# Attention scores leave PSUM through the VectorE instruction that finds their extreme, and the exponential runs in SBUF

## The chip, the cores and the metric

The kernel runs on one NeuronCore of a Trainium2 chip. The metric is the device time of one execution in microseconds (us), as the median of three runs. A core has a matrix engine (TensorE, PE in the profile; its weight loads are PEld), a vector engine (VectorE, DVE), an activation engine (ScalarE, ACT), a general engine (GpSimd, POOL) and a queue engine that issues transfers (SyncE, SP). Each engine works through its own instructions in order; they wait for each other by semaphores. PE writes its results to PSUM, from where DVE and ACT take them; SBUF is the working memory.

## The reference, cut to what matters

```python
# q, k, v: (4, 8, 1152, 64); x is (4, 576, 512)
q_pool = q.reshape(B, H, S // 2, 2, D).mean(axis=3)
scores = (1 / np.sqrt(D)) * np.matmul(q_pool, k.transpose(0, 1, 3, 2))
scores = scores - np.max(scores, axis=-1, keepdims=True)
attn = np.exp(scores)
attn = attn / (np.sum(attn, axis=-1, keepdims=True) + 1e-09)
x = np.matmul(attn, v)            # heads side by side: (4, 576, 512)
xn = (x - mean(x)) / sqrt(var(x) + 1e-06) * g_ln
out = x + np.maximum(xn @ w_ch1, 0.0) @ w_ch2   # 512 -> 2048 -> 512
```

## The kernel before, in words

Heads are handled in 16 pairs. A pair has nine steps (`C = 9`), so there are 144 steps, numbered `i`; a step is one block of 128 pooled queries against all 1152 keys. The operands are split into a high and a low fp16 part, so that three fp16 products stand for one exact one.

Two slots of three PSUM banks hold the scores of two successive steps (`slot(i)`, by `i % 2`). `step(i)` writes out the order of the work by hand, the same for all engines:

- `emit_max(i)`: DVE reduces the 1152 scores of each of the 128 rows to their maximum, `mx` (line 390). From step 36 on DVE also makes `nb`, minus the maximum times the scale (line 395).
- `emit_exp(i)`: ACT takes the scores out of PSUM, scales them by `sc` and adds `nb` as the bias, and writes the exponentials, `pe`, to SBUF in fp32 (line 404). In the first 36 steps (`on_pe`) ACT makes `nb` itself just before (line 401).
- `emit_s(i + 1)`: PE computes the scores of the next step into the other slot (lines 371 and 379).
- In the first 36 steps PE transposes `pe` (`emit_t`, line 437) back into the slot that the scores of the step had, ACT copies the result out in the next step (line 443), and PE multiplies it with the values (`emit_pv`, line 461).
- From step 36 on ACT makes the high part of `pe` (`emit_hi`, line 418) and DVE the low part one step later (`emit_lo`, line 427); in three of nine steps POOL makes the low part instead (lines 240 and 425). A DMA transposes both, and PE multiplies them with the values some steps later (line 470). `pe` has two buffers in turn.

Between these lie the preparation of the next pair (PE transposes of k and q, ACT makes the high part, line 275, DVE the low part, line 272), the conversion of the weights (in the first steps on ACT and DVE, then splits on POOL, lines 240 and 794), and, as soon as rows of x are complete, the units of the dense layers (PE lines 621 and 653, with ACT line 634 and DVE line 635 behind the first). After step 143 only dense layers are left.

`scales(p, ...)` computes the powers of two for a pair; `sc[:, 0:1]` is the factor of the exponential and `sc[:, 1:2]`, for the first four pairs, its negative. `qt` holds the two fp16 parts of the transposed queries.

Of the kernel before, what the change touches and what calls it, by code (L numbers as in the profile page):

```python
# [9 lines left out]
FP32 = mybir.dt.float32  # L10
FP16 = mybir.dt.float16
BF16 = mybir.dt.bfloat16
I32 = mybir.dt.int32
ACTF = mybir.ActivationFunctionType
ALU = mybir.AluOpType
AX = mybir.AxisListType
# [8 lines left out]
def tile_pooled_attention_moe(  # L25
# [18 lines left out]
    nc = tc.nc  # L44
    B, H, S, D = q.shape
# [3 lines left out]
    C = S // 128  # L49
# [13 lines left out]
    const = ctx.enter_context(tc.tile_pool(name="const", bufs=1))  # L63
    raw_p = ctx.enter_context(tc.tile_pool(name="raw", bufs=1))
    tr_p = ctx.enter_context(tc.tile_pool(name="tr", bufs=2))
    p_p = ctx.enter_context(tc.tile_pool(name="pp", bufs=2))
    pt_p = ctx.enter_context(tc.tile_pool(name="pt", bufs=5))
    x_p = ctx.enter_context(tc.tile_pool(name="x", bufs=2))
    sm_p = ctx.enter_context(tc.tile_pool(name="sm", bufs=2))
# [17 lines left out]
    wexp = const.tile([128, 4], FP32, name="wexp")  # L87
    wscl = const.tile([128, 4], FP32, name="wscl")
    inv12 = const.tile([128, 2], FP32, name="inv12")
    both = const.tile([128, 2], FP32, name="nhalf")  # L90
    nhalf, eps = both[:, 0:1], both[0:65, 1:2]

# [30 lines left out]
    def load_q(p, engs):  # L123

        b, hp = divmod(p, HP)
        r = raws[p, "q"] = raw_p.tile([128, C, 2, D], FP32, tag="qr", name="qr", bufs=3)
        for h in range(2):
            engs[h % len(engs)].dma_start(
                out=r[64 * h:64 * h + 64],
                in_=q[b, 2 * hp + h].rearrange("(p c r) d -> p c r d", c=C, r=2),  # L130
            )

    pair = {}

    def state(p):
        if p not in pair:
            pair[p] = {
                x: sm_p.tile([128, 3], FP32, tag=x, name=x, bufs=3)
                for x in ("acc", "e", "s", "sc")
            }  # L140
        return pair[p]
# [9 lines left out]
    def qt_of(p):  # L151
        st = state(p)
        if "qt" not in st:
            st["qt"] = tr_p.tile([128, 2, 1280], FP16, tag="qt", name="qt")
        return st["qt"]

    def pool_q(p, eng):
# [3 lines left out]
    def dup_q(p, eng):  # L161
        x = raws[p, "q"]
        eng.tensor_copy(x[:, :, 1], x[:, :, 0])
# [57 lines left out]
    def scales(p, top, a=0, b=3):  # L221

        st = pair[p]
        e, s, sc = (st[x] for x in ("e", "s", "sc"))
        v = nc.vector
        ei, si = (x.bitcast(I32)[:, a:b] for x in (e, s))
        ti = top.bitcast(I32)
        v.tensor_scalar(ei, ti, EXPO, None, op0=ALU.bitwise_and)
        v.tensor_scalar(si, ti, EXPO, EXPO, op0=ALU.bitwise_and, op1=ALU.bitwise_xor)
        if a == 0:  # L230
            v.scalar_tensor_tensor(
                sc[:, 0:1], e[:, 0:1], 2.0 ** -6, e[:, 1:2], op0=ALU.mult, op1=ALU.mult
            )
            if on_pe(p * C):
                v.scalar_tensor_tensor(
                    sc[:, 1:2], e[:, 0:1], -(2.0 ** -6), e[:, 1:2], op0=ALU.mult, op1=ALU.mult
                )

    def scaled(dst, src, s=1.0):
        nc.gpsimd.tensor_scalar(dst, src, s, 1.0, op0=ALU.mult, op1=ALU.mult)  # L240
# [28 lines left out]
    def split_from(what, ps, s, hi, lo):  # L269

        def low():
            nc.vector.scalar_tensor_tensor(lo, ps, s, hi, op0=ALU.mult, op1=ALU.subtract)  # L272
            have.add(what)

        return (lambda: nc.scalar.activation(out=hi, in_=ps, func=ACTF.Copy, scale=s), low)  # L275
# [31 lines left out]
    def prep_q(p, u):  # L307

        qr, qt, s = raws[p, "q"], qt_of(p), pair[p]["s"]
        ps = bank()  # L310
        z = p % HP // 2
        if u == 2:
            nc.tensor.transpose(ps[:, 0:128], qr[:, C - 1].rearrange("p r d -> p (r d)"), ident)
            o, n = 512, 128
            hi, lo = (qt[:, a, o:o + n] for a in range(2))
            return split_from((p, "q", u), ps[:, 0:n], s[:, 1:2], hi, lo)

        d = (256, 128)[z]
        rows = ps.rearrange("p (a h n) -> p a h n", h=2, n=d)
        for c in range(4):  # L320
            a, n = (0, 64 * c) if z == 0 else (c // 2, 64 * (c % 2))
            nc.tensor.matmul(
                out=rows[:, a, :, n:n + 64], lhsT=qr[:, 4 * u + c].rearrange("p r d -> p (r d)"),
                rhs=ident.rearrange("p (h n) -> p h n", h=2), is_transpose=True, start=True, stop=True,
            )
        if z == 0:

            ps = ps.rearrange("p (h n) -> p h n", h=2)
            hi, lo = (
                qt[:, a, 0:1280].rearrange("p (h n) -> p h n", h=2)[:, :, 256 * u:256 * u + 256]  # L330
                for a in range(2)
            )
        else:
            hi, lo = (qt[:, a, 640 * u:640 * u + 512] for a in range(2))
        return split_from((p, "q", u), ps, s[:, 1:2], hi, lo)
# [9 lines left out]
    def on_pe(i):  # L345

        return 0 <= i < HP * C
# [36 lines left out]
        steps[i] = {"s": sp[:, 0:S]}  # L384

    def emit_max(i):
        st = steps[i]
        mx = sm_p.tile([128, 1], FP32, tag="mx", name="mx")
        nb = st["nb"] = sm_p.tile([128, 1], FP32, tag="nb", name="nb")
        nc.vector.tensor_reduce(mx, st["s"], axis=AX.X, op=ALU.max)  # L390
        sc = pair[i // C]["sc"]
        if on_pe(i):
            st["mx"] = mx
        else:
            nc.vector.tensor_scalar(nb, mx, sc[:, 0:1], -1.0, op0=ALU.mult, op1=ALU.mult)

    def emit_exp(i):
        st = steps[i]
        st["pe"] = p_p.tile([128, S], FP32, tag="pe", name="pe")
        if on_pe(i):  # L400
            nc.scalar.activation(
                out=st["nb"], in_=st["mx"], func=ACTF.Copy, scale=pair[i // C]["sc"][:, 1:2]
            )
        nc.scalar.activation(  # L404
            out=st["pe"], in_=st["s"], func=ACTF.Exp,
            scale=pair[i // C]["sc"][:, 0:1], bias=st["nb"],
        )

    pts = {}

# [131 lines left out]
    def bank():  # L542
        for _ in range(2):
            for _ in free_banks:
                nbank[0] += 1
                n = nbank[1] = free_banks[nbank[0] % len(free_banks)]
                if n not in held and n not in waiting:
                    waiting.add(n)
                    return psum[:, n]
            n = nbank[0] + 1  # L550
            while free_banks[n % len(free_banks)] in held:
                n += 1
            release(free_banks[n % len(free_banks)])
# [504 lines left out]
    with tc.manual_schedule():  # L1058
        def now(fn, *a, **k):
            fn(*a, **k)  # L1060

        load_q(0, (nc.sync, nc.scalar))
        load(0, "k", nc.sync)
        load_q(1, (nc.sync,))
        load(0, "v", nc.sync)
        nc.sync.dma_start(out=gsb, in_=g_ln.rearrange("(k p) -> p k", p=128))
        nc.vector.memset(nhalf, -0.5)
        nc.vector.memset(both[:, 1:2], 0.0)
        nc.vector.memset(both[64:65, 1:2], 1e-9)
        for n in (2, 5):  # L1070
            nc.vector.memset(psum[:, n, 386:387], TINY)
        nc.vector.memset(diag, 0.0)
        nc.vector.memset(ones, 2.0 ** -13)
        nc.scalar.activation(out=wexp[:, 0:1], in_=nhalf, func=ACTF.Exp)
        make_identity(nc, ident)

        warm(110)
        st = state(0)
        nc.vector.memset(st["acc"], 0.0)
        pool_q(0, nc.vector)  # L1080
        dup_q(0, nc.gpsimd)
        bound(0, "q")

        nc.scalar.activation(
            out=kt_of(0).rearrange("p a h n -> p (a h n)")[:, 0:C * D],
            in_=raws[0, "k"][:, 0, 0:C].rearrange("p c d -> p (c d)"), func=ACTF.Abs,
            accum_out=st["acc"][:, 0:1],
        )
        nc.vector.tensor_reduce(
            st["acc"][:, 2:3], raws[0, "k"][:, 1, 0:C], axis=AX.XY, op=ALU.max,  # L1090
            apply_absolute_value=True,
        )
        nc.vector.tensor_tensor(st["acc"][:, 0:1], st["acc"][:, 0:1], st["acc"][:, 2:3], op=ALU.max)
        one, two = all_max(st["acc"][:, 0:2], 2, lambda ps: scales(0, ps, 0, 2))
        one()()
        two()()
        free_banks[:] = [6, 7, 3, 4]
        parts = [fn(0, u) for fn, u in PREPS[0][:3]]
        for hi, lo in parts:
            hi()  # L1100
            lo()
        warm(16)
        emit_s(0)
        preps.extend((fn, 0, u) for fn, u in PREPS[0][3:])
        free_banks[:] = [6, 7]
        for h in range(2):
            take_v(0, h)
        i = 0
        while i < NSTEP + 20 or units or evacs or norms:
            step(i)  # L1110
            i += 1
# [29 lines left out]
```

## Time and profile before

| | |
|---|---|
| median of 3 runs (lowest to highest) | 820.64 us (819.19 to 821.6) |
| the profiled execution, its own time | 819.03 us |
| its span on the core | 816.9 us |
| busy: PE, PEld | 783.9 us (96%), 553.2 us (68%) |
| busy: DVE, ACT, POOL | 611.1 us (75%), 559.9 us (69%), 341.3 us (42%) |

The span runs from the first to the last instruction of the core; 2.1 us of the execution lie outside it. Busy times are unions over an engine's instructions. They are averages over stages that differ: attention steps with PE transposes up to about 175 us, attention steps with DMA transposes and dense units up to about 695 us, dense units alone after that. Ends of matmuls are modelled, so a busy PE isn't a PE at its peak.

### The profile page before, as it was taken

Reading aid. Unit: us, or ns where it says so; the run is one execution under the profiler, and the core shown is the slowest. Engines: PE = TensorE matmul, PEld = TensorE weight load, DVE = VectorE, ACT = ScalarE, POOL = GpSimd, SP = SyncE. Lnnn points to the kernel's source line nnn. Section 1 sums busy time; section 2 is a strip of 40 time slices with the busy share of each in tenths; the row PEclk is TensorE's granted clock in tenths of the full one; section 3 lists DMA queues with packets and bytes.
Section 4 is the critical chain, followed back from the end, with each engine's and each line's share of the span. In section 5 each row is a group of like instructions: output and inputs, shape, how many; then the busy total and the mean of one; then the engine's idle time right before and its main releaser. Section 6 shows DMA issues by size and latency. Waiting matters only on the chain.

```text
span 816.9 us, 21326 instructions
## 1 busy us (share of the span) xinstructions
PE 783.9 (96%) x8978; PEld 553.2 (68%) x8978; DVE 611.1 (75%) x1141; ACT 559.9 (69%) x824; POOL 341.3 (42%) x338
## 2 busy tenths in 40 slices
PE   8899999989989999999999999999999999999997
PEld 7687888767566666657566666666675757766764
DVE  4598999899989887898887888888787877521221
ACT  4899998987786868687868786787778676211010
POOL 2010242389999963475452534527252423200000
PEclk9999999999999999999999999999999999999999
DMA  5837465208699999998998989895979687401001
GB/s 145 246 96 262 155 186 149 72 10 172 114 192 158 183 160 205 171 194 150 204 159 185 172 183 169 166 195 111 227 131 211 127 145 124 79 1 27 14 1 26
DMA packets 276016, 115.94 MB, mean 142 GB/s; under 512 B 259280, under 2 KB 259280, under 8 KB 275920
## 3 DMA queue, kind: packets, MB, share of 16 engines
q1 hardware_dynamic: 275840, 114.29, 68.6%
q8 instruction: 70, 1.15, 0.6%
q10 hardware_dynamic: 80, 0.29, 0.2%
q14 instruction: 26, 0.21, 0.1%
HBM read 46.14 MB, written 4.72 MB: 62 GB/s over the span
## 4 chain that ended last, share of the span: by engine, by line
PE 64%; DVE 16%; ACT 10%; POOL 6%; issue 2%; DMA 2%; SPq 0%; POOLq 0%; ACTq 0%; DVEq 0%
PE psum L653 19%; PE psum L621 18%; PE psum L371 7%; PE psum L470 7%; DVE mx L390 5%; ACT pe L404 4%; DVE hl L427 3%; PE psum L461 3%; PE psum L437 2%; PE psum L379 2%; DVE kt L272 1%; DMA vr<-in_v_dram 1%; ACT pt L443 1%; DVE qr L159 1%; POOL wsl L240 1%
## 5 line engine op out<-in xcount | busy, mean ns | idle before, releaser
L404 ACT ACTIVATE pe<-psum,nb,sc 128x1152 f32<-128x1152 f32 x144 | 188.6, 1309 | 33.6 <-DVE r L518 17.6
L390 DVE TENSOR_REDUCE mx<-psum 128x1 f32<-128x1152 f32 x144 | 194.3, 1349 | 15.5 <-PE psum L470 4.5
L653 PE MATMUL psum<-wsl,ht 128*128 128x512 f16 x864 | 196.6, 379 | 7.0 <-DVE ht L635 4.8
L621 PEld LDWEIGHTS <-wsl 128*128 128x128 f16 x1920 | 169.6, 98 | 19.3 <-issue 1.1
L621 PE MATMUL psum<-xn,wsl 128*128 128x256 f16 x1536 | 176.3, 273 | 0.8 <-DVE ht L635 0.6
L653 PEld LDWEIGHTS <-ht 128*128 128x128 f16 x864 | 81.1, 97 | 95.5 <-issue 7.4
L418 ACT ACTIVATE hl<-pe 128x1152 f16<-128x1152 f32 x108 | 125.6, 1163 | 3.4
L634 ACT ACTIVATE ht<-psum 128x512 f16<-128x512 f32 x72 | 42.8, 595 | 123.4 <-PE psum L621 123.3
L371 PE MATMUL psum<-kt,qt 64*128 64x512 f16 (+1 forms) x960 | 119.9, 381 | 3.9 <-ACT pt L443 1.8
L427 DVE SCALAR_TENSOR_TENSOR hl<-pe,hl 128x1152 f16<-128x1152 f32 x72 | 116.3, 1616 | 0.0
L470 PE MATMUL psum<-vt,pt 128*128 128x65 f16 (+2 forms) x3240 | 106.8, 194 | 0.3 <-DMA pt<-hl 0.2
L470 PEld LDWEIGHTS <-pt 128*128 128x128 f16 (+1 forms) x3240 | 98.3, 100 | 3.2 <-DMA pt<-hl 0.6
L635 DVE SCALAR_TENSOR_TENSOR ht<-psum,ht 128x512 f16<-128x512 f32 x72 | 49.5, 688 | 66.1 <-ACT ht L634 65.7
L240 POOL TENSOR_SCALAR pe<-pe 128x1152 f32<-128x1152 f32 x36 | 43.3, 1204 | 120.1 <-ACT hl L418 120.1
L425 POOL TENSOR_TENSOR hl<-pe,hl 128x1152 f16<-128x1152 f32 x36 | 87.0, 2418 | 3.0
L461 PE MATMUL psum<-pt,vt 128*65 128x128 f32 (+1 forms) x720 | 77.4, 263 | 1.3 <-DVE kt L272 1.3
L461 PEld LDWEIGHTS psum<-pt,vt 128*65 128x65 f32 x720 | 71.4, 138 | 1.6 <-DVE kt L272 1.5
L371 PEld LDWEIGHTS <-qt 64*128 64x128 f16 (+1 forms) x960 | 31.9, 96 | 50.3 <-issue 31.7
L379 PEld LDWEIGHTS <-qt 128*128 128x128 f16 (+1 forms) x320 | 17.5, 99 | 63.0 <-issue 62.8
L246 POOL COPY gate<-gate 128x1 f32<-128x1 f32 x27 | 5.0, 184 | 112.5 <-DVE gate L245 112.5
L272 DVE SCALAR_TENSOR_TENSOR qt<-psum,s,qt 128x512 f16<-128x512 f32 (+1 forms) x48 | 29.5, 614 | 29.6 <-ACT qt L275 28.9
L667 DVE SCALAR_TENSOR_TENSOR xb<-psum,inv,xb 128x512 f32<-128x512 f32 x32 | 23.8, 744 | 35.6 <-PE psum L653 35.5
(115 smaller groups left out, 996.7 us busy)
## 6 DMA issues: line engine op xcount, KB each, us to landing
stage<-in_moe_w_ch_dram SPq DMA_DIRECT2D x32, 512.0 KB, 6.6
kr<-in_k_dram SPq DMA_DIRECT2D x16, 576.0 KB, 4.5
vr<-in_v_dram SPq DMA_DIRECT2D x16, 576.0 KB, 4.9
qr<-in_q_dram SPq DMA_DIRECT2D x31, 288.0 KB, 5.5
out_dram<-xb SPq DMA_DIRECT2D x32, 128.0 KB, 2.4
pt<-hl SPq DMA_TRANSPOSE x108, 5.2
kr<-in_k_dram SPq DMA_DIRECT2D x16, 64.0 KB, 4.2
out_dram<-xh SPq DMA_DIRECT2D x4, 128.0 KB, 2.7
```

The lines of the kernel that those rows point to most:

```text
L240: nc.gpsimd.tensor_scalar(dst, src, s, 1.0, op0=ALU.mult, op1=ALU.mult)
L371: nc.tensor.matmul(out=sp[o:o + w, c0:c0 + 512], lhsT=qt[r:r + 64, qa, q0:q0 + w], rhs=kt[r:r + 64, ka, h], start=(a == 0), stop=(a == 2),)
L390: nc.vector.tensor_reduce(mx, st["s"], axis=AX.X, op=ALU.max)
L404: nc.scalar.activation(out=st["pe"], in_=st["s"], func=ACTF.Exp, scale=pair[i // C]["sc"][:, 0:1], bias=st["nb"],)
L418: nc.scalar.activation(out=hl[:, 0], in_=st["pe"], func=ACTF.Copy, scale=2.0 ** 15)
L425: nc.gpsimd.tensor_tensor(hl[:, 1], st["pe"], hl[:, 0], op=ALU.subtract)
L427: nc.vector.scalar_tensor_tensor(hl[:, 1], st["pe"], 2.0 ** 15, hl[:, 0], op0=ALU.mult, op1=ALU.subtract)
L461: nc.tensor.matmul(out=ps[0:65, q0:q0 + w], lhsT=vt[:, h, c], rhs=pt[:, 128 * u + q0:128 * u + q0 + w], start=(u == 0), stop=(u == C - 1),)
L470: nc.tensor.matmul(out=dst[:, 0:n], lhsT=pt[:, a + u, q0:q0 + w], rhs=vt[:, h, c, x0:x0 + n], start=(u == 0 and a == 0 and n == 65), stop= ...
L621: nc.tensor.matmul(out=ps[:, o:o + n], lhsT=wsl[:, 8 * w + cc, wa, f * 128:f * 128 + 128], rhs=xn[:, xa * KD + cc, 0:n], start=(m == 0), s ...
L635: lambda: nc.vector.scalar_tensor_tensor(lo, pv, 0.0, hi, op0=ALU.max, op1=ALU.subtract),
L653: nc.tensor.matmul(out=ps, lhsT=hv[0][:, ha, f, t * 128:t * 128 + 128], rhs=wsl[:, 8 * w + 4 + f // 2, wa, (f % 2) * DM:(f % 2) * DM + DM] ...
```

## The change

One VectorE instruction (`tensor_tensor_reduce`) reads the scores from PSUM as its first tensor and a zero, repeated along the row, as its second; it adds the two, multiplies by the scale with its sign changed, writes the 1152 results per row to `pe` in SBUF, and writes their minimum to `nb`. It stands where the maximum stood. ACT then computes exp(-1 times `pe` plus `nb`) in SBUF, from `pe` into `pe`. `mx`, the separate computation of `nb` on DVE or ACT, and `sc[:, 1:2]` go. `pe` is now allocated in `emit_max` and has three buffers; the tile for `qt` is shorter by 128 elements a row and its second part is laid out without a gap.

```diff
+    nought = const.tile([128, 1], FP32, name="nought")
...
     def qt_of(p):
         st = state(p)
         if "qt" not in st:
-            st["qt"] = tr_p.tile([128, 2, 1280], FP16, tag="qt", name="qt")
+            x = tr_p.tile([128, 4 * C * 64 + 128], FP16, tag="qt", name="qt")
+            st["qt"] = x[:, 0:4 * C * 64].rearrange("p (a n) -> p a n", a=2)
+            st["qt+"] = x
...
         if a == 0:
             v.scalar_tensor_tensor(
-                sc[:, 0:1], e[:, 0:1], 2.0 ** -6, e[:, 1:2], op0=ALU.mult, op1=ALU.mult
+                sc[:, 0:1], e[:, 0:1], -(2.0 ** -6), e[:, 1:2], op0=ALU.mult, op1=ALU.mult
             )
-            if on_pe(p * C):
-                v.scalar_tensor_tensor(
-                    sc[:, 1:2], e[:, 0:1], -(2.0 ** -6), e[:, 1:2], op0=ALU.mult, op1=ALU.mult
-                )
...
             hi, lo = (
-                qt[:, a, 0:1280].rearrange("p (h n) -> p h n", h=2)[:, :, 256 * u:256 * u + 256]
+                pair[p]["qt+"][:, 1152 * a:1152 * a + 1280].rearrange("p (h n) -> p h n", h=2)[
+                    :, :, 256 * u:256 * u + 256
+                ]
...
     def emit_max(i):
+
         st = steps[i]
-        mx = sm_p.tile([128, 1], FP32, tag="mx", name="mx")
+        st["pe"] = p_p.tile([128, S], FP32, tag="pe", name="pe", bufs=3)
         nb = st["nb"] = sm_p.tile([128, 1], FP32, tag="nb", name="nb")
-        nc.vector.tensor_reduce(mx, st["s"], axis=AX.X, op=ALU.max)
-        sc = pair[i // C]["sc"]
-        if on_pe(i):
-            st["mx"] = mx
-        else:
-            nc.vector.tensor_scalar(nb, mx, sc[:, 0:1], -1.0, op0=ALU.mult, op1=ALU.mult)
+        nc.vector.tensor_tensor_reduce(
+            out=st["pe"], in0=st["s"], in1=nought[:, 0:1].to_broadcast([128, S]),
+            scale=pair[i // C]["sc"][:, 0:1], scalar=3.0e38, op0=ALU.add, op1=ALU.min, accum_out=nb,
+        )
 
     def emit_exp(i):
         st = steps[i]
-        st["pe"] = p_p.tile([128, S], FP32, tag="pe", name="pe")
-        if on_pe(i):
-            nc.scalar.activation(
-                out=st["nb"], in_=st["mx"], func=ACTF.Copy, scale=pair[i // C]["sc"][:, 1:2]
-            )
-        nc.scalar.activation(
-            out=st["pe"], in_=st["s"], func=ACTF.Exp,
-            scale=pair[i // C]["sc"][:, 0:1], bias=st["nb"],
-        )
+        nc.scalar.activation(out=st["pe"], in_=st["pe"], func=ACTF.Exp, scale=-1.0, bias=st["nb"])
...
         nc.vector.memset(nhalf, -0.5)
+        nc.vector.memset(nought, 0.0)
```

## Rows read from the trace of the kernel before

**Rows 1.** Windows: stretch, length, busy us (x instructions) by engine, PEclk, DMA, GB/s

```profile
14.00:170.00 156.00, 149.11 (x1440) 121.83 (x1438) 132.02 (x293) 139.96 (x241) 39.42 (x65) 1.00 0.49 153
170.00:300.00 130.00, 119.80 (x1428) 82.70 (x1425) 118.85 (x198) 99.34 (x137) 120.22 (x90) 1.00 0.81 149
300.00:700.00 400.00, 391.58 (x5069) 261.60 (x5068) 326.21 (x583) 301.30 (x411) 175.50 (x165) 1.00 0.91 169
```

**Rows 2.** The same windows for the maximum alone (line 390, DVE)

```profile
14.00:170.00 156.00, 47.34 (x35) 1.00 0.49 153
170.00:300.00 130.00, 36.34 (x27) 1.00 0.81 149
300.00:700.00 400.00, 110.61 (x82) 1.00 0.91 169
```

**Rows 3.** Timeline of the first stage: start, us, engine, line, [idle before <-releaser]

```profile
89.46 1.35 DVE L390 TENSOR_REDUCE mx<-psum 128x1 f32<-128x1152 f32 x1
...
90.73 0.15 DVE L516 RECIPROCAL r<-psum 64x2 f32<-64x2 f32 x1
90.85 0.29 ACT L401 ACTIVATE nb<-mx,sc 128x1 f32<-128x1 f32 x1 [0.20 <-DVE mx L390]
...
91.18 1.31 ACT L404 ACTIVATE pe<-psum,nb,sc 128x1152 f32<-128x1152 f32 x1
...
93.13 1.15 PE L437 MATMUL psum<-ident,pe 128*128 128x128 f32 x9
...
93.34 0.75 DVE L272 SCALAR_TENSOR_TENSOR kt<-psum,s,kt 128x512 f16<-128x512 f32 x1 [0.31 <-ACT kt L275]
...
94.02 1.35 DVE L390 TENSOR_REDUCE mx<-psum 128x1 f32<-128x1152 f32 x1
```

**Rows 4.** Line 404: first what it waited for, then who waited for it (us, times)

```profile
  POOL hl L425: 7.1, 6
...
  PEld psum L437: 6.1, 9
```

**Rows 5.** Timeline at 228 us, POOL's low part and what follows it

```profile
228.40 2.37 POOL L425 TENSOR_TENSOR hl<-pe,hl 128x1152 f16<-128x1152 f32 x1
...
230.80 1.31 ACT L404 ACTIVATE pe<-psum,nb,sc 128x1152 f32<-128x1152 f32 x1 [1.99 <-POOL hl L425]
...
231.91 1.34 DVE L390 TENSOR_REDUCE mx<-psum 128x1 f32<-128x1152 f32 x1
232.16 0.82 PE L371 MATMUL psum<-kt,qt 64*128 64x512 f16 x6 [0.88 <-ACT pe L404]
```

**Rows 6.** Groups of DVE by form: busy us, mean ns | idle before, releasers

```profile
L635 DVE SCALAR_TENSOR_TENSOR ht<-psum,ht 128x512 f16<-128x512 f32 x72 | 49.5, 688 | 66.1 <-ACT ht L634 65.7
L272 DVE SCALAR_TENSOR_TENSOR qt<-psum,s,qt 128x512 f16<-128x512 f32 x32 | 24.0, 749 | 21.9 <-ACT qt L275 21.6
...
L395 DVE TENSOR_SCALAR nb<-mx,sc 128x1 f32<-128x1 f32 x108 | 23.1, 214 | 3.8
```

**Rows 7.** Line 427: duration in ns, least, median and most

```profile
L427 DVE SCALAR_TENSOR_TENSOR hl<-pe,hl x72: 1347/1350/3133, 184.9 to 691.1; 128x1152 f16<-128x1152 f32 x72
```

**Rows 8.** Timeline at 440 us: DVE's pair, and an ACT instruction with an accumulator

```profile
440.28 1.36 DVE L390 TENSOR_REDUCE mx<-psum 128x1 f32<-128x1152 f32 x1 [1.04 <-PE psum L470]
...
441.80 0.21 DVE L518 TENSOR_SCALAR r<-psum,s 128x1 f32<-128x1 f32 x1
...
446.49 1.15 ACT L179 ACTIVATE kt<-kr 128x1152 f16<-128x1152 f32 x1
...
447.55 0.19 ACT L179 ACTIVATION_READ_ACCUMULATOR kt<-kr 128x1 f32 x1
```

**Rows 9.** Groups of ACT by form: busy us, mean ns | idle before, releasers

```profile
L404 ACT ACTIVATE pe<-psum,nb,sc 128x1152 f32<-128x1152 f32 x144 | 188.6, 1309 | 33.6 <-DVE r L518 17.6 <-POOL hl L425 7.1 <-DVE nb L395 5.6
L418 ACT ACTIVATE hl<-pe 128x1152 f16<-128x1152 f32 x108 | 125.6, 1163 | 3.4
```

**Rows 10.** Windows for line 635 alone (DVE)

```profile
170.00:300.00 130.00, 8.17 (x12) 1.00 0.81 149
```

## The prediction, made before the changed kernel was run

> **What bounds the kernel now.** I read the windows by stage first, because the shares of the whole span mix three kinds of step [rows 1]. From 300 to 700 us PE is busy for 391.6 of 400 us, while DVE has 74 us to spare: whatever the change does to DVE or ACT there can give back at most 8 us and, up to DVE's slack, costs little. After 700 us there are no scores. What can move lies before 300 us. From 14 to 170 us PE is idle for 6.9 of 156 us, and DVE (132) and ACT (140) aren't far behind. From 170 to 300 us PE is idle for 10.2 of 130 us, and DVE (118.9) and POOL (120.2) are the full engines. So the gain of any change to DVE and ACT is bounded by some 17 us of idle PE, and it counts only where a PE wait ends on one of the instructions that it touches.
>
> Next the timeline of one step of the first stage [rows 3]. The reader is to see a loop. DVE finds the maximum at 89.46, ACT makes `nb` and begins the exponential at 91.18, 1.72 us later; ACT then makes the high part of the prepared tile, DVE waits 0.31 us for that and makes the low part at 93.34, and only then, at 94.02, comes the next maximum: a period of 4.56 us, set by neither engine alone. PE, though, transposes at 93.13 without a wait, 0.64 us after the exponential ended at 92.49: here PE is the late one, and a faster loop gives it nothing. The view of line 404's waits says where it would: PE's weight loads waited 6.1 us in 9 places for the exponential before the transposes [rows 4].
>
> Last the waits of the exponential. In six places, 7.1 us, it waited for POOL to give back a buffer of `pe` [rows 4]. One is shown [rows 5]: POOL ends at 230.77, the exponential begins at 230.80, 1.99 us late, and the next scores on PE begin 0.88 us late in their turn, since the exponential still held their PSUM slot.
>
> **The change, part by part.** *The new DVE instruction.* No instruction of this kind is in the trace. Its main part reads 1152 fp32 scores from PSUM and one more input. The reduction takes 47.34/35 = 1.35 us [rows 2]. A three-operand instruction from PSUM with 512 elements takes 0.688 us, the same with a scalar from a tile 0.749 [rows 6], so the scalar costs 0.06; one over 1152 elements takes 1.35 us when nothing stretches it [rows 7]. Main part: 1.35 + 0.06 = 1.41 us. The minimum must then be written out. For that the trace has only ACT's counterpart: 446.49 + 1.15 = 447.64 is the end of the main instruction, 447.55 + 0.19 = 447.74 that of the accumulator's read [rows 8], 0.10 us later. Bounds for the whole: 1.35 us (scalar and read free) and 1.41 + 0.21 = 1.62 us (the read as dear as line 395, with no overlap [rows 6]). I take 1.51, by the ACT read, which is the same act on another engine.
>
> [...]
>
> *What it replaces on DVE.* From step 36 on the pair of maximum and `nb` holds DVE from 440.28 to 441.80, 1.52 us [rows 8]. So DVE is even there: 1.51 for 1.52, within -0.17 and +0.10 a step. In the first 36 steps the next DVE instruction began 1.27 us after the maximum did (89.46 to 90.73 [rows 3]); there DVE pays 0.24 us a step more.
>
> *What it removes on ACT.* In the first 36 steps `nb` goes: from its start to the exponential's is 0.33 us (90.85 to 91.18 [rows 3]). The exponential now reads SBUF with one scalar from a tile. The same length from SBUF without any takes 1.163 us, from PSUM with two 1.309 [rows 9]; these are the bounds, and I take 1.26, nearer the upper, since it keeps its bias: 0.05 us less. ACT is relieved by 0.38 us a step in the first stage and by 0.05 after.
>
> *The loop of the first stage.* Maximum to exponential: 1.72 becomes about 1.51 + 0.06 = 1.57; the exponential gives 0.05 more. The loop goes from 4.56 to 4.36 us. But DVE's own work in that step is 4.56 - 0.31 = 4.25 us, and with 0.24 more it is 4.49. So DVE becomes the limit of such a step, and of the 0.20 only 0.07 is left. Over the stage PE has 149.1/35 = 4.26 us a step and DVE 132.0/35 = 3.77 [rows 1, 2], with the new instruction 4.01: PE stays the fuller engine on average, so DVE's extra work is covered by PE's. If that cover were gone, 35 x 0.24 = 8.4 us would be to pay.
>
> What remains as a gain is where PE waited for the exponential: 9 places, 6.1 us [rows 4]. Each place can give back what the path before it lost: 0.20 by the loop alone, 0.38 where ACT was the full engine. 9 x 0.25 = 2.2 us, with 0.9 and 3.4 as ends; I take off 0.3 for steps in which DVE had no idle time: -1.9 us.
>
> *170 to 300 us.* DVE is even, 27 steps x (-0.17 to +0.10) = -4.6 to +2.7 us, taken as zero. The PSUM slot is now free when DVE is done with it, not after the exponential; the wait of 0.88 us for it goes [rows 5], and the third buffer takes away ACT's waits for POOL, 7.1 us [rows 4], of which little reaches PE, since the exponential's readers have steps to spare. Together -1.0 us, between 0 and -4.
>
> *A wait that is added.* The new instruction must find a free `pe`; behind it on DVE stand the reciprocals for the finished rows and the low parts that PE's dense units read. It needs the buffer of three steps before. In the tight case shown the buffer was given back at 230.77, and the third step's maximum began at 231.91 [rows 5]: 1.14 us to spare, so no price; if POOL's queue were later by more, the 2.37 us of line 425 would be the size of the stall.
>
> *The rest.* One memset, four small DVE instructions less, another layout of `qt` with the same instructions: nothing, hidden in DVE's 24 us of slack in the first stage [rows 1].
>
> *Sum.* -1.9 - 1.0 = -2.9 us against the profiled execution's 819.03: 816.1. The median stands 1.6 us above it, so 820.64 - 2.9 = 817.7 us.
>
> **The rivals.**
>
> *Hidden anyway.* PE has no more than these few waits, and the places that are released early wait next for the dense units' low parts. For it: PE transposes 0.64 us after it could [rows 3]. Against it: nine waits that end on the exponential. Then -0.5 to +1.5 us: 820.9.
>
> *All waits are paid back.* The nine waits (6.1 us) go, and a third of PE's 10.2 idle us from 170 to 300 with them (3.4): -9 us, 811.6. For it: ACT's relief of 0.38 us a step is larger than what most of the waits measure. Against it: DVE takes 0.24 of it back in the same loop.
>
> *Slower: the hand-over of the minimum.* If main part and read together take the upper bound or more, DVE becomes the limit before 300 us. It decides from 1.52 us on in the second stage, where DVE is busy for 91% [rows 1], and from 1.27 + 0.31 = 1.58 on in a regular step of the first. At 1.62: 27 x 0.10 + 26 x 0.04 = 3.7 us (26 are the first stage's 35 less the 9 with a wait), and of the gains about 0.5 left: +3, 823.6. Every further 0.1 us costs some 53 x 0.1 = 5 us. For it: no row of this kind. Against it: the ACT pair overlaps.
>
> *Half rate.* If two inputs, a written result and a running minimum together went at half the elements per unit of time, 1152 x (1.350 - 0.688)/640 = 1.19 us more a step [rows 6, 7]: DVE would be the limit everywhere. 35 x 1.19 + 27 x 1.19 = 74 us before 300 us, less some 25 of DVE's idle 24 + 11 there; after it 82 x 1.19 = 98 less the 74 of slack, of which perhaps half can be used: about +50 + 60, 930 us. Against it: line 427 has two inputs of the same length and is at full rate [rows 7]. [...]
>
> A stretch by POOL, which takes line 427 up to 3.13 us [rows 7], I count with the slower cases at a very small chance: line 635, with one input in PSUM and one in SBUF as the new one has, took 8.17/12 = 0.68 us while POOL was busy for 92% [rows 1, 10], no more than its mean.
>
> **How the numbers follow.** Forecast 0.50, hidden anyway 0.16, all waits paid 0.14, hand-over 0.16, half rate 0.04. The forecast's own range is -0.5 to -5.5 us (the ends of its terms, partly offset): 815.1 to 820.1. A measurement of this kernel tells about 0.3%, 2.5 us, from no change. Three fifths of the forecast lie beyond that, with all of the faster rival: 0.44. Slower: half rate and four fifths of the hand-over: 0.17. Within: 0.39. The range goes from 812, which leaves out half of the faster rival, to 826, which leaves out half rate and the dearer part of the hand-over.
>
> **What the profile after would show.** The new line at about 1.41 us, with a short read right behind it, and 1.5 us from its start to the next DVE instruction; line 404's successor near 1.26 us and no line 401; the exponential 1.57 us after the new instruction's start in the first stage; PE's waits for the exponential down from 6.1 us to about 4; no wait of ACT for POOL's low part, and none of DVE in its place; DVE's busy time from 14 to 170 us up by some 8 us; the stretch from 300 to 700 us unchanged in length. The prediction is wrong if the new instruction with its read takes over 1.6 us, if DVE waits for `pe`, or if PE's idle time before 300 us doesn't fall.

## The result, and the profile after

| | before | after |
|---|---|---|
| median (lowest to highest) | 819.91 us (819.12 to 821.6, 4 runs) | 812.24 us (811.42 to 813.88, 4 runs) |
| the profiled execution, span | 819.03, 816.9 us | 812.92, 811.1 us |

The ratio is 0.9906, with a 95% interval of 0.9881 to 0.9931: the change makes the kernel 7.7 us, or 0.9%, faster. The direction is the one forecast, but the forecast gain was 2.9 us, and 812.24 us lies outside the forecast's own range (815.1 to 820.1). It is inside the stated range, whose fast end is 812, by 0.24 us, and only because half of the faster rival was taken in; that is luck. Runs of one kernel differ by some 1.5 to 2.5 us with their mean granted clock (after, 811.42 us at 1.000, 812.92 at 0.998 and 813.88 at 0.997); at a mean clock of 1.000 the profiled execution before took 819.03 us and two runs after took 811.42 and 811.56 us, which is nearly the same gain.

The windows of the stages after, in the columns of [rows 1]:

```profile
14.00:170.00 156.00, 151.13 (x1456) 123.94 (x1457) 135.28 (x328) 133.40 (x211) 39.87 (x65) 0.99 0.49 153
170.00:300.00 130.00, 119.54 (x1441) 82.23 (x1439) 116.42 (x198) 96.86 (x134) 121.59 (x90) 1.00 0.85 151
300.00:700.00 400.00, 394.72 (x5097) 263.57 (x5094) 316.79 (x590) 295.71 (x412) 175.68 (x169) 1.00 0.92 170
```

Against [rows 1], PE is 2.0 us busier in the first stretch and 3.1 us in the last, and not busier in the middle. The last stretch is the surprise. DVE's busy time rises by 3.3 us in the first stage, where some 8 was expected, and falls by 9.4 us after 300 us.

The new instruction, as a source view of its line (least, median and most ns of one; then the costliest of what it waited for, and who waited for it, in us and times):

```profile
L392 DVE CUSTOM_DVE_ANT_0 pe<-psum,nought,sc x144: 1384/1412/1419, 14.7 to 684.1; 128x1152 f32<-128x1152 f32 x144
L392 DVE DVE_READ_ACCUMULATOR2_ANT nb<- x144: 76/84/89, 16.1 to 685.4; 128x1 f32 x144
...
  PE psum L462: 7.5, 10
...
  ACT pe L399: 31.0, 33
```

Its main part is the 1.41 us of the forecast, with a longest of 1.419: nothing stretches it. It waits mostly for PE's matmuls (the costliest line is that of the matmuls with the values), and nowhere for POOL. The exponential, now line 399, by the same view and with those who waited for it:

```profile
L399 ACT ACTIVATE pe<-pe,nb x144: 1239/1255/1277, 16.2 to 685.6; 128x1152 f32<-128x1152 f32 x144
...
  PEld psum L429: 2.1, 3
```

It takes 1.255 us in the median, where the mean had been 1.309 [rows 9], and PE's weight loads waited 2.1 us in 3 places for it, where it had been 6.1 us in 9 [rows 4]. It waits for DVE alone; POOL's 7.1 us [rows 4] are gone.

One step of the first stage after, on the timeline, to lay beside [rows 3]:

```profile
89.57 1.42 DVE L392 CUSTOM_DVE_ANT_0 pe<-psum,nought,sc 128x1152 f32<-128x1152 f32 x1
90.91 0.09 DVE L392 DVE_READ_ACCUMULATOR2_ANT nb<- 128x1 f32 x1
90.91 0.16 DVE L508 RECIPROCAL r<-psum 64x2 f32<-64x2 f32 x1
91.03 1.26 ACT L399 ACTIVATE pe<-pe,nb 128x1152 f32<-128x1152 f32 x1 [0.17 <-DVE nb L392]
...
93.29 0.75 DVE L271 SCALAR_TENSOR_TENSOR kt<-psum,s,kt 128x512 f16<-128x512 f32 x1
93.97 1.41 DVE L392 CUSTOM_DVE_ANT_0 pe<-psum,nought,sc 128x1152 f32<-128x1152 f32 x1
```

The reader is to see three starts. The read begins at 90.91, before the main part's end at 90.99, and the reciprocal behind it begins at 90.91 too. Before, the reciprocal also began 0.08 us ahead of the end of the maximum (90.73, where 89.46 + 1.35 = 90.81 [rows 3]), so the read takes nothing of its own here. DVE gets on 1.34 us after the new instruction's start, against 1.27 after the old maximum. The exponential begins 1.46 us after that start, against 1.72. And DVE's low part at 93.29 no longer waits for ACT: the period is 4.40 us, against 4.56.

From step 36 on the same hand-over stands against the old pair of 1.52 us [rows 8]:

```profile
442.32 1.41 DVE L392 CUSTOM_DVE_ANT_0 pe<-psum,nought,sc 128x1152 f32<-128x1152 f32 x1
443.66 0.08 DVE L392 DVE_READ_ACCUMULATOR2_ANT nb<- 128x1 f32 x1
443.66 0.22 DVE L510 TENSOR_SCALAR r<-psum,s 128x1 f32<-128x1 f32 x1
```

That is 1.34 us, so DVE gains some 0.18 us in each of 108 steps.

**Where the time went.** Each step starts with line 390 or its successor on DVE. Subtracting those starts on the two timelines gives the gain by stretch (before, steps 5, 36, 63 and 143 start at 36.36, 178.74, 308.29 and 688.72 us; after, at 37.37, 177.06, 306.18 and 684.09). The same subtraction for the experiments below, each against before, in us:

| stretch | after | e3 | e4 | e5 | e6 | e7 | e8 | e9 | e10 | e11 | e12 |
|---|---|---|---|---|---|---|---|---|---|---|---|
| start to step 5 | +1.0 | +2.2 | -0.8 | +1.7 | -0.3 | +0.2 | +0.5 | +1.2 | +1.7 | +1.5 | 0.0 |
| steps 5 to 36 | -2.7 | -2.4 | -2.6 | +0.4 | -2.6 | +0.1 | -2.7 | -2.7 | -2.7 | -2.3 | +0.1 |
| steps 36 to 63 | -0.4 | -0.2 | +0.4 | +0.8 | +0.3 | -0.4 | -4.4 | -4.5 | -2.7 | -0.3 | -1.1 |
| steps 63 to 143 | -2.5 | -2.0 | +0.5 | -2.5 | +0.3 | -2.6 | -2.9 | -4.2 | -2.3 | -2.5 | +0.7 |
| step 143 to the end | -1.2 | -0.1 | -1.1 | -1.1 | +0.1 | -1.2 | -1.1 | -1.1 | -1.2 | -1.1 | +0.3 |

Each column is one profiled execution. Below the first row, stretches that an edit leaves as they were agree with before within some 0.3 us (e6 from step 36 on, e7 up to it), so a difference of that size is not read as an effect.

The first row is mostly the clock. In the profile after, PE's granted clock was 0.57, 0.50, 0.50 and 0.72 in the four microseconds from 26 to 30 us; before, it kept 1.00 there. The window with the fall, after:

```profile
23.90:30.00 6.10, 4.04 (x20) 2.67 (x20) 2.00 (x5) 5.09 (x10) 0.00 (x0) 0.72 0.99 321
```

PE had waited for ACT just ahead of it, for 2.06 us; at the same place before, where the clock held, it had waited for 1.55 us. First after, then before:

```profile
25.74 0.37 PE L372 MATMUL psum<-kt,qt 64*128 64x512 f16 x1 [2.06 <-ACT pt L435]
```

```profile
25.50 0.37 PE L371 MATMUL psum<-kt,qt 64*128 64x512 f16 x1 [1.55 <-ACT pt L443]
```

Why that wait is longer after was not followed up. The profiles of e4 and e6, which have the new instruction in these steps and no such stretch (granted 1.00 in the mean from 14 to 170 us, against 0.99 after), gain 0.3 to 0.8 us in that row. With about -0.5 there, the sum of the column is -7.3 us, near the measured 7.7.

**The last row** has its place on the timeline. Before, the dense unit behind the last exponential waits for it, since it needs a PSUM bank that the exponential still reads:

```profile
690.45 1.31 ACT L404 ACTIVATE pe<-psum,nb,sc 128x1152 f32<-128x1152 f32 x1
...
691.81 2.75 PE L653 MATMUL psum<-wsl,ht 128*128 128x512 f16 x12 [1.07 <-ACT pe L404]
```

After, the same unit begins while the exponential runs:

```profile
685.64 1.25 ACT L399 ACTIVATE pe<-pe,nb 128x1152 f32<-128x1152 f32 x1
...
686.02 2.76 PE L645 MATMUL psum<-wsl,ht 128*128 128x512 f16 x12
```

### The profile page after: what moved, and what is told of

Same layout as the page of the kernel before. It is cut to its first block, busy times and chain, and to the rows that moved or that the text cites. A ratio compares the mean times of both kernels' runs of the same rounds, so it can differ in the third digit from the quotient of the medians.

```text
span 811.1 us, 21365 instructions
## 1 busy us (share of the span) xinstructions
PE 783.1 (97%) x8978; PEld 553.7 (68%) x8978; DVE 599.3 (74%) x1174; ACT 544.4 (67%) x788; POOL 341.3 (42%) x338
## 4 chain that ended last, share of the span: by engine, by line
PE 67%; POOL 13%; DVE 10%; issue 4%; ACT 3%; DMA 2%; SPq 0%; POOLq 0%; ACTq 0%; DVEq 0%
PE psum L645 19%; PE psum L613 18%; PE psum L372 8%; PE psum L462 7%; PE psum L453 5%; POOL wsl L239 4%; PE psum L429 3%; POOL wsl L786 3%; PE psum L380 2%; POOL hl L417 2%; DVE pe L392 2%; DVE hl L419 1%; DMA vr<-in_v_dram 1%; PE psum L321 1%; PE psum L1048 1%
## 5 line engine op out<-in xcount | busy, mean ns | idle before, releaser
L392 DVE CUSTOM_DVE_ANT_0 pe<-psum,nought,sc 128x1152 f32<-128x1152 f32 x144 | 203.1, 1411 | 17.5 <-PE psum L462 7.5
L399 ACT ACTIVATE pe<-pe,nb 128x1152 f32<-128x1152 f32 x144 | 180.4, 1253 | 31.9 <-DVE nb L392 31.0
```

The costliest lines, as they stand in the source:

```text
L392: nc.vector.tensor_tensor_reduce(out=st["pe"], in0=st["s"], in1=nought[:, 0:1].to_broadcast([128, S]), scale=pair[i // C]["sc"][:, 0:1], s ...
L399: nc.scalar.activation(out=st["pe"], in_=st["pe"], func=ACTF.Exp, scale=-1.0, bias=st["nb"])
```

## The experiments

The pieces to tell apart are the third buffer, the place that the exponential reads (and with it the early release of PSUM), DVE's hand-over, and ACT's `nb`. Diffs are against the changed kernel unless another is named. Each time stands against runs of the kernel before on the same chip (820.7, 820.38 or 819.35 us).

### e1: two buffers of `pe`

```diff
-        st["pe"] = p_p.tile([128, S], FP32, tag="pe", name="pe", bufs=3)
+        st["pe"] = p_p.tile([128, S], FP32, tag="pe", name="pe", bufs=2)
```

> The changed kernel with two buffers for pe instead of three; all else stays. If the third buffer is itself a source of the gain (theory B), half of the 7.7 us is lost: about 816 us. My theory is that the buffer is no gain of its own but a condition: the new instruction takes its buffer at the start of a step, where the exponential took it in the middle, so with two it must wait on DVE for POOL's low part of two steps before. By the times of the trace of before POOL ended that part after the maximum of that step had begun in most of the 36 places, by about 1 us and by up to 5; so DVE would wait some 30 us in all, part of it hidden behind PE: 822 to 840 us, slower than before.

833.62 us (832.59 to 834.9), ratio 1.0165 [1.0149, 1.0181]: slower than before by 13 us. DVE's waits, and the second window:

```profile
DVE pe L392 <- POOL hl L417: 35.6, 22, 5.9
```

```profile
170.00:300.00 130.00, 114.97 (x1316) 78.83 (x1316) 99.56 (x185) 89.59 (x125) 107.00 (x83) 0.95 0.76 140
```

With two buffers it is DVE that waits for POOL's low part, 35.6 us in 22 places, where ACT had waited 7.1 us in 6 [rows 4], and from 170 to 300 us DVE gets through 99.6 us of work, against 116.4 in the changed kernel. PE, busy for 115.0 us there against 119.5, was granted 0.95 of its clock in the mean. The third buffer is a condition of the change.

### e2: three buffers alone

Against the kernel before (with the shorter `qt` of the change; `mx` and `nb` share a tile, for room):

```diff
-        st["pe"] = p_p.tile([128, S], FP32, tag="pe", name="pe")
+        st["pe"] = p_p.tile([128, S], FP32, tag="pe", name="pe", bufs=3)
```

> The kernel before with a third buffer for pe (and the shorter qt that makes room for it), the maximum and the exponential as before. Theory B: 3 us or more faster than before. My theory: ACT's waits for POOL (7.1 us, 6 places) go, but little reaches PE: 0 to 1.5 us faster, not to be told from no change.

819.87 us, ratio 0.9997 [0.9988, 1.0005]: nothing. ACT's 7.1 us for POOL were hidden, as the forecast held for most of them, and the profile has none of them left. By the interval at most 0.12%, 1.0 us, could come from here.

### e3: the exponential from PSUM, as before

```diff
-        nc.scalar.activation(out=st["pe"], in_=st["pe"], func=ACTF.Exp, scale=-1.0, bias=st["nb"])
+        nc.scalar.activation(
+            out=st["pe"], in_=st["s"], func=ACTF.Exp,
+            scale=pair[i // C]["sc"][:, 1:2], bias=st["nb"],
+        )
```

(`sc[:, 1:2]` is the scale with a positive sign. DVE's instruction is unchanged, its written scores unused.)

> The changed kernel, but the exponential reads the scores from PSUM with a positive scale, as before, so it holds the PSUM slot until it ends and takes 0.05 us more; the copy that the new instruction writes is overwritten unread. One small DVE instruction more for each pair. Theory R (the slot that is released early, and the shorter exponential, bring the gain): 3 us or more of the 7.7 are lost, 815 or above. Theory D (DVE's time brings it): under 1 us is lost, 812 to 813.

815.77 us (813.69 to 816.11), 0.994 [0.9926, 0.9954]: by the ratios some 2.8 of the 7.7 us are lost (the 3.5 us of the next run's expectation compare times of two chips). The timeline at its last exponential:

```profile
687.83 1.31 ACT L402 ACTIVATE pe<-psum,nb,sc 128x1152 f32<-128x1152 f32 x1
...
689.19 2.75 PE L651 MATMUL psum<-wsl,ht 128*128 128x512 f16 x12 [1.01 <-ACT pe L402]
```

The dense unit's wait at the end is back, 1.01 us for 1.07, and each other run whose late exponentials read PSUM has it as well (e2, e6 and e12, 1.1 us each); it is absent from every profile in which they read SBUF. So this 1.1 us is shown to come from the bank's early release. Another 1.0 us is spread over the steps (the table), in amounts of 0.2 to 0.5 that hardly stand out. That makes 2.1 us for the edit; the rest of this profile's loss is in its first row, where its clock was the lower one (0.99 granted from 14 to 170 us, 0.997 in the mean).

### e11: the exponential in SBUF, but as long as from PSUM

```diff
-        nc.scalar.activation(out=st["pe"], in_=st["pe"], func=ACTF.Exp, scale=-1.0, bias=st["nb"])
+        nc.scalar.activation(out=st["pe"], in_=st["pe"], func=ACTF.Exp, scale=nought[:, 1:2], bias=st["nb"])
```

(`nought[:, 1:2]` holds -1.)

> The changed kernel with the exponential's factor -1 taken from a tile: it still works in SBUF, but should take about as long as out of PSUM (1.31 us) or up to 1.35. The kernel with the exponential out of PSUM lost 3.5 us. If its longer exponential was the cause, this one loses 3 us or more: 815 to 816. If the slot that is held was the cause, under 1 us: 812 to 813.

813.91 us (812.23 to 816.14), 0.9927 [0.9912, 0.9941]. The group of the exponential (busy us, mean ns):

```profile
L399 ACT ACTIVATE pe<-pe,nb,nought 128x1152 f32<-128x1152 f32 x144 | 193.9, 1347 | 31.0 <-DVE nb L392 30.3
```

It is now longer than before's 1309 ns [rows 9], and yet, outside the first row of the table, it loses 0.6 us where e3 loses 2.1 (0.4 of them from step 5 to 36, and 0.1 at most where e3 loses 1.1, at the end). e3's loss is therefore not mainly one of the exponential's duration; the held bank is the larger part. That rests on one profile of each, since the intervals of the two times overlap.

### e4: DVE's time given back from step 36 on

```diff
-            scale=pair[i // C]["sc"][:, 0:1], scalar=3.0e38, op0=ALU.add, op1=ALU.min, accum_out=nb,
+            scale=pair[i // C]["sc"][:, 0:1], scalar=3.0e38, op0=ALU.add, op1=ALU.min, accum_out=nb if on_pe(i) else mn,
         )
+        if not on_pe(i):
+            nc.vector.tensor_scalar(nb, mn, nought, 1.0, op0=ALU.add, op1=ALU.mult)
```

> The changed kernel with a small DVE instruction behind the new one from step 36 on, which takes the minimum to nb: DVE is again as long as with the pair of before (about 0.2 us a step more, 20 us in all). Theory D: 3 us or more of the gain are lost, 815 to 817. Theory R: under 1 us is lost.

816.89 us (814.98 to 817.48), 0.9961 [0.9948, 0.9975]: some 4 us are lost. The group of the added instruction, then the last window:

```profile
L399 DVE TENSOR_SCALAR nb<-nb,nought 128x1 f32<-128x1 f32 x108 | 23.1, 214 | 3.9
```

```profile
300.00:700.00 400.00, 391.81 (x5068) 261.92 (x5067) 332.25 (x669) 295.71 (x411) 175.24 (x166) 1.00 0.92 169
```

PE falls back to before's 391.6 us [rows 1], and in the table the gain of steps 63 to 143 turns from -2.5 into +0.5, while the stages that the edit does not touch keep theirs. So what comes back after 300 us, apart from the end, hangs on these 0.21 us a step on DVE between the scores and the exponential. With them the hand-over from step 36 on is about as long as the forecast had it, and the gain of the whole is 3.8 us, near its 2.9. The edit adds occupancy and delay at once, and this run does not separate them.

### e5: ACT's `nb` given back in the first 36 steps

```diff
+        nb = st["nb"]
+        if on_pe(i):
+            nb = st["nb2"]
+            nc.scalar.activation(out=nb, in_=st["nb"], func=ACTF.Copy, scale=nought[:, 1:2])
-        nc.scalar.activation(out=st["pe"], in_=st["pe"], func=ACTF.Exp, scale=-1.0, bias=st["nb"])
+        nc.scalar.activation(out=st["pe"], in_=st["pe"], func=ACTF.Exp, scale=-1.0, bias=nb)
```

(Here `nought[:, 1:2]` holds 1.)

> The changed kernel with a small ACT instruction before the exponential in the first 36 steps, like the one that made nb there before: ACT is again 0.3 us a step longer in the first stage. If ACT's relief there brought the drop of PE's waits for the exponential (6.1 to 2.1 us), 2 to 4 us of the 7.7 are lost: 814 to 816. If the shorter path over DVE did it, under 1 us.

820.35 us (818.03 to 822.87, 12 runs), 1.0002 [0.9991, 1.0014]: the whole gain is lost, more than either theory had. What the profile shows of it is smaller: steps 5 to 36 lose 3.1 us against the changed kernel, steps 36 to 63 1.2, and PE's weight loads wait again for the exponential:

```profile
PEld psum L435 <- ACT pe L405: 5.4, 8, 1.1
```

That is near before's 6.1 us in 9 places [rows 4], so the removal of ACT's `nb` from the path is what frees the first stage. (The edit makes ACT busier and the path longer at once; which of the two counts is not separated.) The profiled execution, 818.03 us, is this kernel's fastest, with a mean clock of 0.997; most of the others have 0.996, one 0.994, while the kernel before has 0.998 or 1.000. So the time holds both the longer first stage and more of the lower clock. Why this edit brings more of the lower clock was not followed up.

### e6 and e7: the change in the first 36 steps alone, and from step 36 on alone

```diff
+    def fused(i):
+        return on_pe(i)
```

(That is e6; e7 has `not on_pe(i)`. Where `fused` does not hold, the maximum, `nb` and the exponential from PSUM stand as before; three buffers throughout.)

> The new instruction and the exponential in SBUF only in the first 36 steps; from step 36 on the maximum, nb and the exponential out of PSUM as before (three buffers all along). In the profile of after the steps begin 1.7 us earlier than before by step 36, and the span is 5.8 us shorter. If the gain lies by stage as those starts say, this kernel is 1.5 to 3 us faster than before: 818 to 819. If the first stage has most of it, as my sum had it (1.9 of 2.9), 5 us or more: 815 or below.

> The other half of the split: the new instruction and the exponential in SBUF only from step 36 on, the first 36 steps as before. The kernel with the first half alone was 2.6 us faster than before (ratio 0.9968). If the halves add up, this one is 5 us faster: 815 to 816. If they need each other, less than 3.5 us: 817 or above.

e6: 817.34 us (816.39 to 818.37), 0.9968 [0.9956, 0.998]. e7: 816.17 us (814.76 to 819.21, 12 runs), 0.9961 [0.9948, 0.9973]. In the table each keeps its own stretches and has nothing in the other's. The halves add up to 0.32% + 0.39% = 0.71%; the whole has 0.94%, with an interval from 0.69% on. By its time e7's gain of 3.2 us lies on the side of "they need each other" (under 3.5 us); but its runs differ in their mean clock (0.996 to 1.000), and by the profiles the spans of the two halves, 2.2 and 3.9 us shorter, add up to the whole's 5.8.

### e8, e9, e10: POOL's low parts moved to DVE

POOL is busy for 121.59 of 130 us from 170 to 300 us, and after the change it has a larger share of the chain that ended last. Shares by engine, before:

```profile
PE 64%; DVE 16%; ACT 10%; POOL 6%; issue 2%; DMA 2%; SPq 0%; POOLq 0%; ACTq 0%; DVEq 0%
```

After:

```profile
PE 67%; POOL 13%; DVE 10%; issue 4%; ACT 3%; DMA 2%; SPq 0%; POOLq 0%; ACTq 0%; DVEq 0%
```

So the change's freed DVE time was offered to the low parts that POOL makes in three of nine steps: up to step 63 (e8), in all steps (e9), and up to step 63 for one of the three (e10).

```diff
-        return i % C in (2, 5, 8)
+        return i % C in (2, 5, 8) and i >= 63                 # e8
+        return i % C in (2, 5, 8) and i >= 144                # e9
+        return i % C in ((2, 8) if i < 63 else (2, 5, 8))     # e10
```

> The changed kernel with all low parts of steps 36 to 62 on DVE; POOL makes them from step 63 on as before. POOL was busy for 94% from 170 to 300 us and stands in the chain that ended last with 13%; nine of its low parts (3.6 us each) go to DVE (1.35 us each, 12 us in all, where DVE has 13.6 us of 130 idle). If POOL bounds that stage in the changed kernel, 2 to 4 us faster than it: 808 to 810. If DVE does, 3 us or more slower: 815 or above.

> The changed kernel with all 36 low parts of POOL on DVE. From 300 to 700 us DVE had 83 us idle and takes 27 x 1.35 = 36 us more. If DVE's time still counts there, as the kernel with 0.2 us a step given back says (it lost 4 us for 20 us of DVE), this is 3 to 7 us slower than the kernel with the early ones alone (808.4): 811 to 815. If POOL's stretch of DVE's own low parts was the cost, as fast or faster: 806 to 808.

> The changed kernel with one of three of POOL's low parts of steps 36 to 62 on DVE (three in all), the rest as in the changed kernel. If POOL's load in that stage sets the time in proportion, a third of the 3.9 us that all nine gave: about 811. If one place sets it, all or nothing: 808 or 812.

e8: 808.38 us (806.84 to 809.66), 0.9858 [0.9842, 0.9873]. e9: 807.71 us (807.4 to 807.85), 0.9854 [0.9841, 0.9868]. e10: 811.74 us (808.9 to 812.98), 0.99 [0.9883, 0.9917]. By these times e10 has no gain over the changed kernel that can be told, but its profile has one: from step 36 to 63 it stands at -2.7 us where the changed kernel has -0.4 and e8 -4.4, so one of three moved gives more than half of what all three give. Its first row (+1.7 us, in a profile with a mean clock of 0.997) hides part of that; its one run at a mean clock of 1.000 took 808.9 us, against 811.42 and 811.56. The second window of e8, then the last of e9:

```profile
170.00:300.00 130.00, 123.17 (x1474) 83.92 (x1475) 123.34 (x212) 100.09 (x139) 96.43 (x75) 1.00 0.84 156
```

```profile
300.00:700.00 400.00, 396.55 (x5133) 266.57 (x5130) 347.47 (x619) 295.21 (x412) 80.71 (x112) 1.00 0.90 169
```

In e8 POOL loses 25 us of work there and DVE takes only 7 more, and PE gains 3.6 us: the stretch that the change itself hardly moved moves by 4.4 us against before. In e9 DVE has 31 us more after 300 us than in the changed kernel and PE is busier all the same. That is the side of e9's second theory, and DVE's own low parts are indeed shorter there (1.62 us in the mean in the changed kernel, 1.47 in e9, 1.35 in the median of both); whether that or POOL's lighter load brings the gain is not separated. Both beat both kernels; e9 is the fastest version of this study, 1.5% under the kernel before.

### e12: the same move without the change

Against the kernel before:

```diff
-        return i % C in (2, 5, 8)
+        return i % C in (2, 5, 8) and i >= 63
```

> The kernel before with all low parts of steps 36 to 62 on DVE, nothing else changed. If the freed DVE time of the new instruction is what makes room for them, this gains under 1.5 us or loses: 819 or above. If POOL was the bound in both kernels, it gains about as much as in the changed one, 3 to 4 us: 816 to 817.

818.86 us (817.72 to 821.19, 12 runs), 0.9989 [0.9978, 1.0001]. Its second window:

```profile
170.00:300.00 130.00, 121.83 (x1438) 83.94 (x1434) 122.57 (x204) 100.02 (x138) 94.63 (x75) 0.99 0.79 149
```

By its time the same edit is worth nothing that can be told in the kernel before (0.22% at most), and 3.9 us in the changed one. DVE is as full as in e8 (122.6 and 123.3 us), but in e8 that holds more of the work: 27 steps at 0.18 us less are 4.9 us. The profile shows what became of the move here: it gains 1.1 us from step 36 to 63 and gives 1.0 back after it, and within the gain lies a loss. One of DVE's low parts, beside POOL's work on the weights, lasts 3.32 us; PE waits 1.79 us for the DVE instruction behind it, and the granted clock is 0.66 and 0.50 in the two windows that follow:

```profile
210.77 3.32 DVE L427 SCALAR_TENSOR_TENSOR hl<-pe,hl 128x1152 f16<-128x1152 f32 x1
...
215.33 0.63 PE L576 MATMUL psum<-ident,xs 128*128 128x128 f32 x4 [1.79 <-DVE qt L272]
```

```profile
216.00:218.00 2.00, 2.00 (x30) 1.46 (x27) 1.97 (x4) 1.85 (x2) 1.92 (x3) 0.66 1.16 213
218.00:220.00 2.00, 2.00 (x14) 0.91 (x12) 1.97 (x4) 1.97 (x5) 2.00 (x1) 0.50 0.14 30
```

PE is busy throughout these two windows, so the lower clock costs some 1.7 us (an estimate from these two rows, which takes PE's work to go with the granted clock: 2 x 0.34 + 2 x 0.50). Eleven of e12's twelve runs have a mean clock of 0.994 to 0.998, where 14 of the 23 runs before have 0.999 or 1.000. So in this stretch part of the difference between the profiles of e8 and e12 is the clock, and not room on DVE alone; e8's runs have 0.996 to 0.999, so how much of the difference in time is the clock's stays open. The third buffer and the early release differ as well between the two, so which of these makes the room is not shown.

## Why the prediction came out as it did

The direction, the place of the first gain and most single prices held; the sum was too small by 4.8 us, and that the time is still within the stated range is luck, by 0.24 us.

- *The new instruction's main part*: 1.41 us forecast, 1.412 measured. Neither half rate nor a stretch by POOL appears in 144 instances (1384 to 1419 ns).
- *Its hand-over*: 1.51 us forecast, 1.34 measured, under the lower bound of 1.35. This is the term that was mis-sized. The forecast laid the accumulator's read behind the main part, by ACT's pair [rows 8]. On DVE the read takes 0.08 us, starts 0.06 to 0.09 us before the main part has ended, and the next instruction starts with it. The 0.10 us that the sum had for a read on DVE no run shows; the trace after has the read, in all 144 steps, as a second instruction that keeps DVE no longer (1.34 us to the next instruction, with a main part of 1.41). So DVE pays 0.07 us a step in the first stage and not 0.24, and gains 0.18 a step later where the forecast had it even (its lower bound was -0.17).
- *The first stage*: -1.9 us forecast; -2.7 us measured from step 5 on, and some -0.5 before it. PE's waits for the exponential fell to 2.1 us, not to 4. The forecast's own argument gave it too little, because with 1.51 us DVE would have become the limit of a step (4.49 us); with 1.34 the step shown is 4.40. e5 shows that taking ACT's `nb` out of the path is the part that matters there. The lower end of this term, 0.9 us, follows from neither of its own figures (9 x 0.20 = 1.8, 9 x 0.07 = 0.6).
- *170 to 300 us*: -1.0 us forecast, -0.4 measured. ACT's waits for POOL were indeed hidden (e2), and DVE's gain of 4.9 us did not reach PE. In e8, with POOL's low parts moved, that stretch gains 4.4 us; how much of it is DVE's freed time stays open (e12).
- *After 300 us*: nothing forecast, -2.5 us in the steps and -1.2 at the end measured. The bound "at most 8 us" held; the step that failed is the choice of zero under it, since a DVE step taken as even left nothing to come back. PE's idle 8.4 us were treated as out of reach, but most of them end on DVE: before, of 8.3 us of listed waits from 300 to 700 us, 5.4 are for DVE and 2.5 for ACT. The first three lines (us, times, longest) are

```profile
PE psum L653 <- DVE ht L635: 2.2, 2, 1.3
PE psum L653 <- DVE xb L667: 1.1, 1, 1.1
PE psum L653 <- ACT pe L404: 1.1, 1, 1.1
```

and after, the first two have become (the third is gone)

```profile
PE psum L645 <- DVE ht L627: 1.6, 2, 1.0
...
PE psum L645 <- DVE xb L659: 0.8, 1, 0.8
```

  All listed waits sum to 8.3 us before and 5.1 after; those for DVE fell from 5.4 to 3.6. e4 shows that the 2.5 us hang on the shorter DVE step, and e3 that the third wait, 1.1 us at the end of attention, was one for PSUM. The forecast had seen that release, and had priced it at one place only [rows 5].
- *The third buffer*: no price and no gain of its own, as forecast (e2); that it must be there is e1.
- *The exponential*: 1.26 us forecast, 1.255 measured; 1.57 us after the new instruction's start forecast, 1.46 measured, again by the read. No line 401, no wait of ACT for POOL, and none of DVE in its place, as listed.

Of the rivals, "all waits are paid back" has nearly the size (811.6 us), but not the mechanism: half of the gain lies after 300 us, where it had nothing, and PE's idle time from 170 to 300 us did not fall.

Of the theories weighed in the runs, that of DVE's time and that of the earlier release of PSUM both hold in part: e4 shows the first (2.5 us after step 63), e3 against e11 the second (1.1 us at the end; the 1.0 us at most in the steps is near what two profiles differ by). Neither covers the first stage, which hangs on ACT's `nb` (e5).

What stays open: whether e4 loses by DVE's occupancy or by the later exponential (e9 adds 31 us to DVE after 300 us without a loss, which speaks for the delay, but takes POOL's low parts out as well); which of the changes lets e8 gain what e12 does not, and how much of that is the clock; and why e5 brings more of the lower clock.

## What to carry to other kernels

For an instruction that joins several, work out when the next instruction on its engine and the first consumer can start, not only how long it lasts: here that difference (1.34 against 1.51 us) was most of the forecast's error, as e4 shows, which puts it back from step 36 on and gains 3.8 us. A few us of idle time on the bounding engine are worth listing by what ends them, even in a stage where it is 98% busy: most of those waits ended on the engines that the change relieved. And when an edit frees time on one engine, offer it work from a neighbour that now stands on the chain: the same move was worth 3.9 us with the change, and without it nothing that can be told, where an instruction stretched to 3.32 us and a granted clock of 0.66 and 0.50 over 4 us took back part of it.

## What the runs showed of the hardware that was not expected

- The read of DVE's accumulator took 76 to 89 ns and began 1.34 us after the start of a main part of 1.41 us (medians of 144). In the two places shown the next DVE instruction began with it, 0.08 and 0.07 us ahead of the main part's end; behind the old maximum one began 0.08 us ahead [rows 3]. ACT's counterpart lasted 0.19 us [rows 8].
- In e11 the exponential of 1152 elements, with its scale taken from a tile in place of a constant, was some 94 ns longer (means of 1253 and 1347 ns), which is more than the 56 ns between the old one from PSUM (1309 [rows 9]) and the new one in SBUF.
- In e1, where DVE waited 35.6 us for POOL's low part, the mean granted clock from 170 to 300 us was 0.95, and PE's busy time 115.0 us, against 1.00 and 119.5 in the changed kernel. In the run's mean the clock was 0.986.
